# Turning the state by four full transposes, one half for both heads, and an earlier second half of the merge

## The chip, the cores and the metric

The kernel runs on one core of a Trainium2 chip. A core has a matrix engine (TensorE, "PE" in the profile, with its weight loads as "PEld"), three engines for element work (VectorE "DVE", ScalarE "ACT", GpSimd "POOL"), and SyncE ("SP"), from whose queue nearly all transfers of this kernel are issued. Each engine works through its own list of instructions; semaphores tie the lists together. The metric is the device time of one execution in microseconds, lower being better. TensorE writes its results to PSUM[...]; the other data live in SBUF.

## The reference, cut to what matters

The first half is a linear attention with a state of 40 x 40 per head (4 batches, 8 heads, 768 steps); the second is a mixture of four small networks, applied to the first half's output, all in float32:

```python
for t in range(S):
    y[:, :, t] = np.einsum('bhd,bhde->bhe', rt, state)
    Sa = np.einsum('bhde,bhe->bhd', state, at)
    state_decay = state * wt[:, :, None, :] - np.einsum('bhd,bhe->bhde', Sa, bt)
    state = state_decay + np.einsum('bhd,bhe->bhde', vt, kt)
...
p = domain_probs / (domain_probs.sum(-1, keepdims=True) + 1e-09)
for e in range(E):                      # 4 networks
    h = np.maximum(x @ w1[e], 0.0)      # (3072, 320) @ (320, 1024)
    out += p[:, e:e + 1] * (h @ w2[e])  # (3072, 1024) @ (1024, 320)
```

## The kernel before, in words

**Tiling.** Time is cut into 12 chunks of 64 steps. A *unit* is one chunk of two batches, so there are 24; two units in a row share a chunk. Inside a chunk the recurrence is written with matrices: scores between the 64 steps, a triangular system that is inverted, and the carried state. The 8 heads form four pairs (index j, head s within the pair), the two batches are index i, so a product has 16 blocks of up to 64 x 64. `quadrants` (L370) issues these on the four 64 x 64 quarters of TensorE, in an order given as a list of (j, s, i). A float32 matmul shows as two records in the profile, a transpose as one.

**Stages of a unit.** They are Python generators, advanced by the main loop with `run(generator, n)`:

- `within` (L389), two units ahead. The decays are turned and multiplied up (G, L400 to L410); pg turns them (L416); gp is its scaled reciprocal (L418, L419); n_tok and k_tok (L455, L459) are b and k scaled by it; A, V and R are turned 32 x 32 on VectorE (AT, VT, RT, by L228); pNT and pKT (L441) turn n_tok and k_tok; pc (L448) has the scores of values and receptances, pfe and pe those of a, n and k; EV (L516) is a first right-hand side.
- `substitute` (L523) inverts 32 x 32 triangles. VectorE makes M (L534 to L550) from copies of F (L528), then for all but the first two units GpSimd runs 48 steps on Z (L559, L572). That is the longest serial piece in a unit.
- `merge` (L578) joins two 32 x 32 inverses to one of 64 x 64. Its first part turns Z to Qc and QTc on VectorE (L583, L585) and copies to QT on GpSimd (L591); then pY (L609) with four ScalarE copies to Yq, then pQ (L612) with four to QT (L606).
- `step` (L615) carries the state. prn holds two results in the same two PSUM banks: the state times AT, added to EV to give RH (L633), and the state turned (psn, by products with the identity), which ScalarE copies to SN (L638). Then psat and its copies SaT, SX (L654, L659); pxr and its copies RS (L679); pdy, which gives the outputs Y (L694, L699) and the new state (L704, L705). From the third chunk on Y goes to xT, the input of the mixture, by twelve DMAs on SP's queue (L723).

**The mixture.** `mixture_of_chunk` (L836) puts pieces on a list: up-projections (ph, L738 for the last 64 rows of the weights in 64 x 64 quarters, L752 for the rest, ScalarE's hs L757, with w1 pieces reloaded from memory each time into w1p) and down-projections (p, L873, seven products in place of eight, from sums of hs on VectorE, a, L867; weighted sums osb L773). The main loop (L1057) runs four stretches of a unit's steps, and after each calls `gap(n)`, which takes up to two pieces off that list, so that TensorE has mixture work while other engines work on the recurrence. `lead()` issues the L738 part of the next up-projection ahead of its piece.

**What sets the order.** Inside an engine's list, a tile scheduler decides by its own estimate of times, except where `tc.keep_in_program_order` pins an instruction to its place in the program. The matmuls' results share a ring of five PSUM banks (`big`, L72) and one of three ("mm"); a matmul into a bank waits until the bank's last reader is done.

**The steady main loop before the change** (u from 5): pe, pxr; gap 0; pg, pev, pdy; gap 1; pNT, pKT, pc, prn with both results, pY; gap 2; pQ, pfe, the lead, psat; substitution of the next unit begins; gap 3. In terms of what stands around the change, from L1097: `run(w, 2)` (pNT to pc), `run(s_next, 1)` (prn), `run(m, 1)` (pY), `gap(2)`, `run(m, 1)` (pQ).

**Where a pair's heads stand.** Turned values and receptances have 128 partitions: in one half of 64 stands one head's 40 numbers, in the other another's. Before, `d_half(j, s)` (L357) puts head s of pair j in half s XOR (j mod 2), so the two heads of a pair lie in different halves, and `of_d_half` picks slots 0 and 3, or 1 and 2, of each group of four.

## Time and profile before

| | before |
|---|---|
| median of 3 runs | 1132.29 us (1129.44 to 1134.07) |
| profiled execution | 1129.6 us |
| its span on the core | 1127.5 us |
| granted TensorE clock, mean | 0.986 |
| TensorE busy (matmuls / weight loads) | 1083.1 us (96%) / 963.2 us (85%) |
| VectorE, GpSimd, ScalarE busy | 758.8, 498.8, 353.0 us |
| memory traffic | 111.79 MB read, 3.93 MB written |

The rows of the page come from one profiled execution. A row of the groups or of the timeline has the line of the program, the engine, the operation, the tile written and those read, sizes, and how often; in brackets, or after the last bar, stands the idle time of that engine just before, with what ended it. Rows of waits read "who waits <- for whom: us in total, times, longest us". Matmuls are pipelined: the length of one record says less than the distance between two starts.

### The profile page before, as it was taken

What the parts mean: (1) busy time and instruction counts of PE and PEld (TensorE: products, weight loads), DVE (VectorE), ACT (ScalarE), POOL (GpSimd) and SP (SyncE); (2) the same over time, 40 slices, a digit from 0 to 9 for tenths busy, and PEclk for the clock granted to TensorE, in tenths of its full rate; (3) what the DMA queues carried; (4) which work ended last, traced back from release to release, by engine and by line L of the source; (5) the groups of instructions that cost most, each with busy time, mean ns of one, the idle gap of its engine ahead of it and who ended that gap; (6) DMA issues with size and microseconds to landing.
All of it is one profiled execution on the core that took longest, in us unless ns stands there. A gap on an engine that the chain in (4) does not pass through costs nothing.

```text
span 1127.5 us, 38551 instructions
## 1 busy us (share of the span) xinstructions
PE 1083.1 (96%) x16100; PEld 963.2 (85%) x16100; DVE 758.8 (67%) x1553; ACT 353.0 (31%) x956; POOL 498.8 (44%) x1272
## 2 busy tenths in 40 slices
PE   6899997999999999999999999999999999999998
PEld 5777776788989889988989989989899999888887
DVE  8766547797766767677677677677677686553343
ACT  2323423332332332432432332332333323321110
POOL 5005727754625526437437347346346356340000
PEclk7899998999999999999999999999999999999999
DMA  7784553245253543644543543544553442231320
GB/s 118 214 239 125 130 113 71 71 108 126 77 130 88 122 102 99 141 103 93 143 104 88 143 103 90 142 96 96 133 114 86 122 110 63 76 90 57 108 90 12
DMA packets 268868, 122.18 MB, mean 108 GB/s; under 512 B 213736, under 2 KB 242072, under 8 KB 268696
## 3 DMA queue, kind: packets, MB, share of 16 engines
q1 hardware_dynamic: 265416, 119.12, 43.4%
q8 instruction: 127, 2.08, 0.8%
q10 hardware_dynamic: 3280, 0.61, 0.3%
q14 instruction: 45, 0.37, 0.1%
HBM read 111.79 MB, written 3.93 MB: 103 GB/s over the span
## 4 chain that ended last, share of the span: by engine, by line
PE 67%; POOL 10%; DVE 7%; issue 4%; ACT 2%; SPq 1%; DMA 1%; DVEq 0%; POOLq 0%
PE p L873 23%; PE ph L752 22%; PE ph L738 7%; POOL Z L572 6%; POOL Z L559 4%; PE pdy L376 2%; PE psat L376 2%; PE po L796 2%; DVE M L534 1%; PE pxr L376 1%; PE prn L376 1%; PE pQ L599 1%; PE pfe L376 1%; DVE G L406 1%; PE pc L376 1%
## 5 line engine op out<-in xcount | busy, mean ns | idle before, releaser
L752 PE MATMUL ph<-xT,w1p 128*128 128x256 f32 (+1 forms) x1520 | 342.7, 378 | 1.7 <-issue 1.7
L752 PEld LDWEIGHTS ph<-xT,w1p 128*128 128x128 f32 x1520 | 273.4, 190 | 63.1 <-issue 25.6
L572 POOL TENSOR_TENSOR Z<-Z 128x31 f32<-128x31 f32 (+7 forms) x704 | 257.2, 365 | 55.2
L867 DVE TENSOR_TENSOR a<-hs 128x512 f32<-128x512 f32 x220 | 153.8, 716 | 104.6 <-ACT hs L757 104.6
L559 POOL TENSOR_TENSOR Z<-M,Z 128x62 f32<-128x62 f32 (+7 forms) x352 | 144.0, 409 | 134.5 <-DVE M L550 108.7
L757 ACT ACTIVATE hs<-ph 128x512 f32<-128x512 f32 (+1 forms) x208 | 115.3, 564 | 235.3 <-PE ph L752 234.3
L873 PE MATMUL p<-sums,a 128*128 128x160 f32 x1056 | 165.1, 299 | 0.0
L873 PEld LDWEIGHTS p<-sums,a 128*128 128x128 f32 x1056 | 152.9, 190 | 2.3
L773 DVE SCALAR_TENSOR_TENSOR osb<-p,gate,osb 128x320 f32<-128x320 f32 (+1 forms) x243 | 107.9, 482 | 55.3 <-PE p L873 52.1
L531 POOL COPY below<-F 32x256 f32<-32x256 f32 x48 | 23.4, 488 | 219.5 <-ACT F L489 217.8
L738 PE MATMUL ph<-xT,w1p 64*64 64x256 f32 (+1 forms) x1520 | 111.1, 379 | 5.4 <-issue 5.4
L873 PE MATMUL p<-w,a 128*128 128x160 f32 x704 | 105.8, 301 | 0.9 <-ACT hs L757 0.5
L873 PE MATMUL p<-w,hs 128*128 128x160 f32 x704 | 102.9, 299 | 0.0
L873 PEld LDWEIGHTS p<-w,hs 128*128 128x128 f32 x704 | 100.3, 190 | 2.2
L873 PEld LDWEIGHTS p<-w,a 128*128 128x128 f32 x704 | 98.3, 190 | 3.6 <-ACT hs L757 3.6
L591 POOL COPY QT<-QTc 32x256 f32<-32x256 f32 x96 | 49.3, 513 | 91.4 <-DVE QTc L585 44.9
L738 PEld LDWEIGHTS ph<-xT,w1p 64*64 64x64 f32 x1520 | 66.1, 135 | 14.3 <-issue 9.8
L534 DVE STREAM_TRANSPOSE M<-blocks 128x1024 f32<-128x1024 f32 x24 | 47.2, 1968 | 33.9 <-ACT blocks L528 33.7
L679 ACT COPY RS<-pxr 64x256 f32<-64x256 f32 x88 | 32.2, 366 | 115.0 <-DVE SX L387 73.6
L419 DVE RECIPROCAL gp<-gp 128x320 f32<-128x320 f32 x24 | 51.7, 2153 | 0.8
L516 ACT COPY EV<-pev 64x160 f32<-64x160 f32 x96 | 23.4, 286 | 88.1 <-PE pev L376 87.7
L583 DVE STREAM_TRANSPOSE Qc<-Z 128x256 f32<-128x256 f32 x24 | 15.1, 631 | 49.1 <-POOL Z L572 48.9
(151 smaller groups left out, 1427.9 us busy)
## 6 DMA issues: line engine op xcount, KB each, us to landing
w1p<-in_moe_w_dram SPq DMA_DIRECT2D x95, 512.0 KB
w1p<-in_moe_w_dram SPq DMA_DIRECT2D x190, 64.0 KB
w<-in_moe_w_dram SPq DMA_DIRECT2D x4, 1280.0 KB
sums<-in_moe_w_dram SPq DMA_DIRECT2D x9, 512.0 KB
natW<-in_w_dram SPq DMA_DIRECT2D x48, 80.0 KB
natB<-in_b_dram SPq DMA_DIRECT2D x48, 80.0 KB
natK<-in_k_dram SPq DMA_DIRECT2D x48, 80.0 KB
out_dram<-osb SPq DMA_DIRECT2D x46, 80.0 KB
```

The lines of the kernel that those rows point to most:

```text
L376: nc.tensor.matmul(out=p[row][half(col), lo + at * out_cols:lo + (at + 1) * out_cols], lhsT=lhsT, rhs=rhs, start=(n == 0), stop=(n == len( ...
L419: pin(nc.vector.reciprocal(out=gp[:], in_=gp[:]))
L534: ins = nc.vector.transpose(out=M[:], in_=cols)
L559: ins = eng.tensor_tensor(out=Z[:, 1:3, 0:n, j + 1:Q], in0=M[:, j:j + 2, None, j + 1:Q].to_broadcast([P, 2, n, m]), in1=Z[:, here, 0:n, j: ...
L572: eng.tensor_tensor(out=z[:, 0], in0=z[:, 0], in1=z[:, x], op=ALU.add)
L591: ins = nc.gpsimd.tensor_copy(out=q.QT[quarter(i), :, quarter(i % 2)], in_=QTc[quarter(i)])
L738: nc.tensor.matmul(out=ph[i][half(c), f, :], lhsT=w1.last[part(i), f, half(c)], rhs=xT[part(i), 2, :], start=(f == 0), stop=False,)
L752: nc.tensor.matmul(out=ph[i][:, f, :], lhsT=w1.main[:, g, at * P:(at + 1) * P], rhs=xT[:, g, :], start=False, stop=(g == 1 and f == HF // ...
L757: nc.scalar.activation(out=h[:, i * HF // 2:(i + 1) * HF // 2, 0:n], in_=ph[i][:], func=ACTF.Relu,)
L773: nc.vector.scalar_tensor_tensor(out=to, in0=p, scalar=sc, in1=to, op0=ALU.mult, op1=ALU.add)
L867: nc.vector.tensor_tensor(out=t[:], in0=x, in1=y, op=op)
L873: nc.tensor.matmul(out=p[:, n * HD:(n + 1) * HD], lhsT=a[:, f, :], rhs=b[:, f, :], start=(f == 0), stop=(f == HF - 1),)
```

## The change

Four edits, with what follows from them in the tiles:

1. The carried state is turned by four float32 transposes of 128 x 128 (`turn_state`), one for two pairs of one batch, instead of sixteen quarter matmuls with the identity. They are issued after pg, in the stretch before the unit's own, into one PSUM bank of their own; one ScalarE copy of 128 x 512 makes SN (a tile with one buffer of its own) in place of two of 128 x 256. The ring "step" falls from three buffers to two.
2. Both heads of a pair of turned values and receptances (and of what is multiplied with them) lie in the same half: the half is j mod 2, the slot 2 (j div 2) + s. The loads, pc, psat, pxr and the masks follow; the copies of pxr to RS become two of 128 partitions in place of four of 64. In the first three units, where V and R are turned on TensorE, there are four copies each in place of three.
3. For u from 5, pY and prh (the rest of prn) are issued ahead of pc, and pQ is issued before gap 2 in place of after it.
4. A `lead()` puts the L738 part of gap 2's up-projection ahead of pQ.

The diff, cut to its core:

```diff
@@ load_raw
-                    sets = ((slice(0, 8, 2), slice(r, 16, 4)), (slice(1, 8, 2), slice(3 - r, 16, 4)))
+                    sets = [(slice(y, 8, 2), slice(2 * r + y, 16, 4)) for y in range(2)]
@@ helpers
-    def d_half(j, s):
-        return s ^ (j % 2)
+    def of_d(x, j, s, i, n=64):
+        return x[64 * (j % 2):64 * (j % 2) + n, 4 * i + 2 * (j // 2) + s, :]
...
-    BY_PAIRS = [(2 * j + x, s, i) for i in range(2) for j in range(2) for s, x in QUADS]
+    BY_D_TOKENS = [(2 * jj + r, s, i) for jj in range(2) for s in range(2) for r, i in QUADS]
+    BY_TOKENS_D = [(2 * jj + x, s, r ^ s) for jj in range(2) for s in range(2) for r, x in QUADS]
+    BY_D_HEADS = [(2 * jj + r, s, i) for jj in range(2) for i in range(2) for r, s in QUADS]
@@ before step
+    def turn_state(q):
+
+        if q.start:
+            return
+        psn = big("psn")
+        for i in range(2):
+            for jj in range(2):
+                x = state[q.b[i]][:, 2 * jj:2 * jj + 2, :].rearrange("p j d -> p (j d)")
+                at = (2 * i + jj) * P
+                nc.tensor.transpose(out=psn[:, at:at + P], in_=x, identity=ident[:])
+        q.SN = sb.tile([P, 2, 2, 2, 64], FP32, name="SN", tag="SN", bufs=1)
+        nc.scalar.copy(out=q.SN[:].rearrange("p i jj s e -> p (i jj s e)"), in_=psn[:])
@@ step
-            psn = quadrants(p, NJ * D, BY_PAIRS, 64, lambda j, s, i: (
-                s, d_half(j, s), 2 * i + j // 2, st[i][half(s), j, :], ident[half(s), half(s)],
-            ))
...
-            SN = sb.tile([P, 2, 2 * 2, 64], FP32, name="SN", tag="step", bufs=3)
-            for s in range(2):
-                nc.scalar.copy(out=SN[:, s], in_=psn[s])
...
             for x in range(2):
-                for s in range(2):
-                    nc.scalar.copy(
-                        out=RS[half(s), x ^ s::2], in_=prs[x][half(s)].rearrange("p (j i) t -> p j i t", i=2),
-                    )
+                nc.scalar.copy(out=RS[:, x::2], in_=prs[x].rearrange("p (jj i) t -> p jj i t", i=2))
@@ main loop
         run(w, 1)
+        if u + 1 < NU:
+            turn_state(units[u + 1])
         if not early:
             run(w_next)
         run(s)
...
-        run(w, 2)
+        run(w, 1)
+        if not early:
+            run(m, 1)
+            run(s_next, 1)
+        run(w, 1)
...
         if early:
             run(m, 1)
         else:
-            run(s_next, 1)
+            lead()
             run(m, 1)
         if soon:
             substitute(units[u + 2], nc.gpsimd)
         gap(2)
 
-        if not early:
-            run(m, 1)
         if not soon:
             run(w, 1)
```

More of the change, by code (lines that the diff above doesn't have):

```diff
@@ L355, in head @@
         return 2 * j + s
-    def d_half(j, s):
-        return s ^ (j % 2)
+    def of_d(x, j, s, i, n=64):
+        return x[64 * (j % 2):64 * (j % 2) + n, 4 * i + 2 * (j // 2) + s, :]
     def of_d_half(x, r):
-        return x.rearrange("p (jj four) e -> p jj four e", four=4)[:, :, slice(1, 3) if r else slice(0, 4, 3), :]
+        return x.rearrange("p (jj four) e -> p jj four e", four=4)[:, :, 2 * r:2 * r + 2, :]
     BY_TOKENS = [(j, s, i) for j in range(NJ) for s, i in QUADS]
-    BY_PAIRS = [(2 * j + x, s, i) for i in range(2) for j in range(2) for s, x in QUADS]
+    BY_D_TOKENS = [(2 * jj + r, s, i) for jj in range(2) for s in range(2) for r, i in QUADS]
+    BY_TOKENS_D = [(2 * jj + x, s, r ^ s) for jj in range(2) for s in range(2) for r, x in QUADS]
+    BY_D_HEADS = [(2 * jj + r, s, i) for jj in range(2) for i in range(2) for r, s in QUADS]
     def banks(name):
@@ L428, in turn_rv @@
                 p = turn(f"p{x}T", tok(n["padded" + x]), q.u == 1)[:].rearrange("p (j i t) -> p j i t", i=2, t=L)
-                to = t[:].rearrange("p (i j) t -> p j i t", i=2)
-                nc.scalar.copy(out=to[:, 0::2], in_=p[:, 0::2])
+                to = t[:].rearrange("p (i jj s) t -> p s jj i t", i=2, s=2)
                 for r in range(2):
-                    nc.scalar.copy(out=to[half(r), 1::2], in_=p[half(1 - r), 1::2])
+                    for y in range(2):
+                        nc.scalar.copy(out=to[half(r), y], in_=p[half(y), r::2])
             return VT
@@ L447, in causal_scores @@
         def causal_scores(VT):
-            pc = quadrants(banks("pc"), 0, BY_TOKENS, L, lambda j, s, i: (
-                d_half(j, s), i, j, of_slots(VT, d_half(j, s), j, i, D), of_slots(q.RT, d_half(j, s), j, i, D),
+            pc = quadrants(banks("pc"), 0, BY_D_TOKENS, L, lambda j, s, i: (
+                j % 2, i, 2 * (j // 2) + s, of_d(VT, j, s, i, D), of_d(q.RT, j, s, i, D),
             ))
@@ L622, in step @@
         else:
-            p = banks("prn")
-            prh = quadrants(p, 0, BY_TOKENS, D, lambda j, s, i: (
+            prh = quadrants(banks("prh"), 0, BY_TOKENS, D, lambda j, s, i: (
                 s, i ^ s, j, of_slots(q.AT, s, j, i), st[i][half(s), j, 0:D],
-            ))
-            psn = quadrants(p, NJ * D, BY_PAIRS, 64, lambda j, s, i: (
-                s, d_half(j, s), 2 * i + j // 2, st[i][half(s), j, :], ident[half(s), half(s)],
             ))
@@ L635, in step @@
                 )
-            SN = sb.tile([P, 2, 2 * 2, 64], FP32, name="SN", tag="step", bufs=3)
-            for s in range(2):
-                nc.scalar.copy(out=SN[:, s], in_=psn[s])
         yield
         p = banks("psat")
-        psa = quadrants(p, 0, BY_TOKENS, L, lambda j, s, i: (
-            i ^ s, d_half(j, s), j, RH[half(i ^ s), head(j, s), :], q.QT[half(i ^ s), head(j, s), :],
+        psa = quadrants(p, 0, BY_TOKENS_D, L, lambda j, s, i: (
+            i ^ s, j % 2, 2 * (j // 2) + s, RH[half(i ^ s), head(j, s), :], q.QT[half(i ^ s), head(j, s), :],
         ))
@@ L651, in step @@
             ))
-        SaT = sb.tile([P, NJ, 2, L], FP32, name="SaT", tag="step", bufs=3)
+        SaT = sb.tile([P, NJ, 2, L], FP32, name="SaT", tag="step", bufs=2)
         for x in range(2):
@@ L662, in step @@
         p = banks("pxr")
-        px = quadrants(p, 0, BY_TOKENS, L, lambda j, s, i: (
-            d_half(j, s), i, j, SaT[half(d_half(j, s)), j, i ^ s, :], of_slots(q.RT, d_half(j, s), j, i),
+        px = quadrants(p, 0, BY_D_TOKENS, L, lambda j, s, i: (
+            j % 2, i, 2 * (j // 2) + s, SaT[half(j % 2), 2 * (j // 2) + s, i ^ s, :], of_d(q.RT, j, s, i),
         ))
         if not q.start:
-            prs = quadrants(p, NJ * L, BY_PAIRS, L, lambda j, s, i: (
-                d_half(j, s), s, 2 * (j // 2) + i, SN[half(d_half(j, s)), s, 2 * i + j // 2, :],
-                of_slots(q.RT, d_half(j, s), j, i),
+            prs = quadrants(p, NJ * L, BY_D_HEADS, L, lambda j, s, i: (
+                j % 2, s, 2 * (j // 2) + i, q.SN[half(j % 2), i, j // 2, s, :], of_d(q.RT, j, s, i),
             ))
@@ L675, in step @@
         if not q.start:
-            RS = sb.tile([P, NJ, 2, L], FP32, name="RS", tag="step", bufs=3)
+            RS = sb.tile([P, NJ, 2, L], FP32, name="RS", tag="step", bufs=2)
             for x in range(2):
-                for s in range(2):
-                    nc.scalar.copy(
-                        out=RS[half(s), x ^ s::2], in_=prs[x][half(s)].rearrange("p (j i) t -> p j i t", i=2),
-                    )
+                nc.scalar.copy(out=RS[:, x::2], in_=prs[x].rearrange("p (jj i) t -> p jj i t", i=2))
         yield
@@ L690, in step @@
         )
-        Y = sb.tile([P, NJ, 2, L], FP32, name="Y", tag="step", bufs=3)
+        Y = sb.tile([P, NJ, 2, L], FP32, name="Y", tag="step", bufs=2)
         Gv = q.G.rearrange("p (j i) t -> p j i t", i=2)
```

## The prediction

> **What bounds the kernel now.** I read the page first, parts 1, 2 and 4.

> ```profile
> PE 1083.1 (96%) x16100; PEld 963.2 (85%) x16100; DVE 758.8 (67%) x1553; ACT 353.0 (31%) x956; POOL 498.8 (44%) x1272
> PE   6899997999999999999999999999999999999998
> PE 67%; POOL 10%; DVE 7%; issue 4%; ACT 2%; SPq 1%; DMA 1%; DVEq 0%; POOLq 0%
> ```

> TensorE is full after the first fifth, and most of the ending chain is its own work: matmuls run back to back, so each microsecond it waits in the steady part is added to the time. Next the waits, for what is just in time.

> ```profile
> ACT SN L638 <- DVE RH L633: 74.6, 21, 5.4
> DVE Qc L583 <- POOL Z L572: 48.9, 20, 6.0
> PE pY L599 <- DVE QTc L585: 5.8, 4, 3.4
> ```

> VectorE waits some 2.4 us per unit at the head of its queue for GpSimd's substitution (Z) before it can transpose it (Qc); TensorE hardly notices. Why shows on the timelines of TensorE and then VectorE (start, length, what).

> ```profile
> 561.53 0.60 PE L340 MATMUL pg<-ident,G 128*128 128x128 f32 x4
> 562.06 0.68 PE L376 MATMUL pev<-VC,ET 64*64 64x40 f32 x32
> ...
> 571.94 0.60 PE L340 MATMUL pNT<-ident,n_tok 128*128 128x128 f32 x4
> 572.38 0.60 PE L340 MATMUL pKT<-ident,k_tok 128*128 128x128 f32 x4
> 572.91 0.70 PE L376 MATMUL pc<-RT,VT 40*64 40x64 f32 x32
> 573.42 0.63 PE L376 MATMUL prn<-state,AT 64*64 64x40 f32 x32
> 573.86 0.67 PE L376 MATMUL prn<-ident,state 64*64 64x64 f32 x32
> 574.36 0.57 PE L599 MATMUL pY<-QTc,below 64*64 64x64 f32 x13
> ```

> I time a unit from the start of pg. pNT starts at 10.41 in every steady unit, pc at 11.38, pY at 12.83; units take 42.74 to 43.24. In the unit whose pg starts at 604.39, VectorE did:

> ```profile
> 608.54 0.66 DVE L228 STREAM_TRANSPOSE RT<-rawR 128x512 f32<-128x512 f32 x1
> 609.12 0.72 DVE L694 TENSOR_TENSOR Y<-pdy,RS 128x256 f32<-128x256 f32 x2
> ...
> 611.36 0.48 DVE L455 SCALAR_TENSOR_TENSOR n_tok<-natB,gp 128x320 f32<-128x320 f32 x1
> ...
> 612.09 0.65 DVE L459 TENSOR_TENSOR k_tok<-natK,gp 128x320 f32<-128x320 f32 x1
> 615.13 0.64 DVE L583 STREAM_TRANSPOSE Qc<-Z 128x256 f32<-128x256 f32 x1 [2.39 <-POOL Z L572]
> 615.62 0.41 DVE L228 STREAM_TRANSPOSE G<-rawW 128x256 f32<-128x256 f32 x1
> 615.94 0.40 DVE L585 STREAM_TRANSPOSE QTc<-Qc 128x256 f32<-128x256 f32 x1
> ```

> n_tok, which pNT needs, ends at 7.45; k_tok at 8.35; Qc starts at 10.74, when Z is done; QTc ends at 11.95, before pY. Nothing that TensorE needs before pY stands behind Qc.

> [...]the 2.39 us at Qc agrees, later instructions did not overtake it. [...]the trace has 0.39 us of "issue" idleness where 128x128 ph loads follow 64x64 ones, and 32 records per unit for the state turned in quadrants against four for a 128x128 transpose. [...]in the trace the Z steps under n_tok and k_tok run 0.33, 0.23 and 0.13 us over their usual pitch.

> **The change, part by part.** *State.* Sixteen quadrant matmuls, 32 records, go: 573.86 to 574.36, 0.50 us per unit. Four transposes are added; pNT to pKT gives four in 0.44. They stand beside pg[...]: -0.06. But psn's PSUM bank passes to the second bank of pdy (this is in the built order and its waits), which now waits for ScalarE's copy of 128x512 (0.59, the row of KT). psn ends 1.04 after pg, the copy at 1.67, pdy's second bank is due at 1.55: +0.2. Behind it on TensorE stand pdy and the up-projection; ScalarE was idle there, so its queue (the EV copies, needed much later) may slip 0.6 at no cost.

> *Halves.* R and V are loaded with as many DMAs of the same sizes on SP's queue. The RS copies fall from four of 366 ns to two, off TensorE's path: 0, hidden by 8 us that ScalarE idled before RS. Units 0 to 2 get one ScalarE copy more for each of V and R: 6 x 0.37, at most 2 us, partly hidden.

> *Merge and SN.* SN no longer stands between Yq and hs in ScalarE's queue behind RH; p26 then no longer waits for hs. pfe came at 22.66 in three steady units and 22.88 to 23.22 in the rest, so -0.3. pQ's eight matmuls only move, and Yq (four copies, 1.09) is ready: pY 12.0 to 12.4, copies 12.7 to 13.8, pQ due at 14.2. Its copies to QT go ahead of hs instead of ahead of F: 0. Per unit: -0.06 + 0.2 - 0.3, about -0.2; over 13 steady units -2.6.

> *The order on VectorE.* The built order of the changed kernel differs in seven units, every second one from the unit of 432.78 on:

> ```
> before: gp reciprocal RT Y Y state Y state state n_tok state k_tok Qc G QTc
> after:  gp reciprocal RT Qc Y Y state Y state state n_tok state k_tok QTc
> ```

> Qc is hoisted over everything that pNT needs, while Z is no earlier. Z starts from M, which follows psat by 3.9 us through ScalarE's copies (24.34 to 28.25), lasts 25.4 with its start-up, and pg follows psat by 18.5: Z ends at 3.9 + 25.4 - 18.5 = 10.8 however the unit shifts. Take off the 0.69[...], since VectorE now idles there: 10.1. Qc starts then, Y 0.5 later, n_tok ends 2.72 after that (609.12 to 611.84): 13.3. pNT is due at 10.41 + 0.44 + 0.2 = 11.05, so TensorE stands 2.25. k_tok ends 0.9 later, at 14.2; pKT is due at 13.75: 0.48 more. QTc (14.55) is in time for pY (14.75). Seven times 2.73 is 19.1.

> What is late next: Y, so its twelve xT DMAs on SP, and w1p behind them.

> ```profile
> 610.82 9.36 SPq L723 DMA_DIRECT2D xT<-Y  x12
> 620.29 1.66 SPq L287 DMA_DIRECT2D w1p<-in_moe_w_dram  x3
> ```

> xT starts 1.70 after Y: 12.25; w1p is issued at 21.7. The matmuls on it are due at 22.7 + 0.5 + 2.7 = 26.0, 4.3 us later. The tightest such pair before was 5.9 without a stall, and one w1p in the chain took 4.70: 0 to 1.6, I take 0.3, seven times, +2. xT itself lands in time, as do natB, natK and rawW behind it, needed a unit later.

> In four of the other units RT now stands before Y; its last DMA is issued at 4.3 to 4.9 there and must land, k_tok shifts to 11.2 to 12, Qc with it, and pY, due at 12.0 now, waits about 0.5: 4 x 0.5, and 0.1 in two more, +2.2. If RT's data are early this is 0.6 in all.

> Sum: -2.6 + 19.1 + 2 + 2.2 = +20.7, and 0 +- 3 for the first 430 us, where other waits (DMA, VectorE) rule. On the profiled execution of 1129.6 (its span of 1127.5 plus 2.1) this gives 1150.3; it lies 2.7 under the median of 1132.29, so on medians 1153.

> **Rivals.** *The wait is hidden.* If Qc's new place costs nothing, only the small gains remain: about -0.2 in 20 units, 1128. Z would have to end by 11.05 - 2.72 - 0.5 = 7.8 for that, 3 us before any steady unit shows it; for this, only that the order was chosen at all. This is the other side, and it decides at 7.8.

> *The wait is smaller.* [...]a delayed unit gives back part of its stall: 1.2 us per stall instead of 2.7, 1142. The trace speaks against a return: from pY on TensorE is full.

> *The clock drops.* [...]The trace shows both: after 2.2 us of idleness at 179.5 the 128x128 transposes took 421 ns for 275, after 2.3 at 369.2 nothing changed. A half-clock spell costs some 1.7 us (the windows of 100 to 200 us lose 3 at a clock of 0.97). In all seven: +11, 1164.

> *w1p is late.* 1.6 in each of seven, with the upper ends of RT: +10, 1163. That the change does not do what it says is no case: the built order has the four transposes, two RS copies and pQ ahead of the up-projection.

> **How the numbers follow.** Qc's place as worked out 0.66; smaller 0.12; hidden or faster 0.09; clock 0.09; w1p 0.04. The predicted time is that of the first, 1153, its own range 1147 to 1159 (stall 2.0 to 3.4). The 8 in 10 reach to 1138 and 1163. Half a per cent, 5.7 us, is what a measurement tells here: faster than 1126.6 gets 0.06, within 0.09 (some of "hidden", the edge of "smaller"), slower 0.85.

> **What would show it.** In the changed profile the wait of pNT and pKT for VectorE's n_tok and k_tok should read some 19 us in seven pairs, Qc's wait for Z lengthen to about 5 us in those units, and psn's four transposes take 0.44. Waits of pdy for ScalarE's SN should be 0.1 to 0.3 each; pY for QTc a few in the RT units. If pNT never waits, the forecast is wrong; if units without Qc hoisted don't get 0.2 shorter, the gains are.

## The result, and the profile after it

The changed kernel takes 1158.01 us in the median of 6 runs (1156.21 to 1161.31), the kernel before 1133.24 beside it (6 runs, 1129.44 to 1135.38). The ratio is 1.0226, with a 95% interval of 1.0203 to 1.0248: slower by 2.3%, 24.8 us. The prediction was 1153, with 1138 to 1163 as its range. The profiled execution took 1160.05 us, with a span of 1157.9 against 1127.5 before and a mean TensorE clock of 0.979 against 0.986.

First the page of the changed kernel: part 1, the TensorE slices of part 2, and the engines in the chain that ended last.

```profile
PE 1095.9 (95%) x15484; PEld 973.5 (84%) x15484; DVE 757.1 (65%) x1553; ACT 339.0 (29%) x896; POOL 492.1 (43%) x1272
PE   6799997999999998999999999999999999999998
PE 54%; POOL 19%; DVE 8%; issue 5%; ACT 2%; DMA 2%; SPq 1%; DVEq 0%; POOLq 0%
```

TensorE has 616 records fewer and still takes 30 us longer. The slices hide that, since one of them covers 29 us; the chain does not: GpSimd's Z went from 10% to 19% of it, TensorE from 67% to 54%. The waits (engine and line that waited, what it waited for, us in all, times, longest) say where:

```profile
ACT SN L628 <- PE psn L626: 75.0, 21, 4.6
DVE Qc L585 <- POOL Z L574: 58.8, 20, 5.6
...
PE pNT L340 <- DVE n_tok L457: 15.1, 9, 2.3
...
PE pY L601 <- DVE QTc L587: 5.9, 7, 2.2
...
PE ph L741 <- DMA w1p<-in_moe_w_dram: 3.5, 4, 1.9
```

SN no longer waits for RH, but for its own psn. Qc waits 10 us more for Z in all, and two waits have appeared that the prediction named: pNT for n_tok, and ph for its weights. The unit whose pg starts at 616.36 shows both. TensorE's timeline (start, length, what, and in brackets the idle time before it and its releaser):

```profile
616.36 0.60 PE L340 MATMUL pg<-ident,G 128*128 128x128 f32 x4
616.79 0.60 PE L626 MATMUL psn<-ident,state 128*128 128x128 f32 x4
617.32 0.68 PE L378 MATMUL pev<-VC,ET 64*64 64x40 f32 x32
...
629.29 0.66 PE L340 MATMUL pNT<-ident,n_tok 128*128 128x128 f32 x4 [1.69 <-DVE n_tok L457]
630.01 0.63 PE L340 MATMUL pKT<-ident,k_tok 128*128 128x128 f32 x4
```

The four transposes cost 0.43 (pev starts 0.96 after pg, for 0.53 before). pNT starts at 12.93 after pg. In the units that do not stall it starts at 11.07. VectorE in the same unit:

```profile
621.29 0.66 DVE L228 STREAM_TRANSPOSE RT<-rawR 128x512 f32<-128x512 f32 x1
626.33 0.62 DVE L585 STREAM_TRANSPOSE Qc<-Z 128x256 f32<-128x256 f32 x1 [4.39 <-POOL Z L574]
626.81 0.72 DVE L697 TENSOR_TENSOR Y<-pdy,RS 128x256 f32<-128x256 f32 x2
...
628.75 0.48 DVE L457 SCALAR_TENSOR_TENSOR n_tok<-natB,gp 128x320 f32<-128x320 f32 x1
...
629.38 0.48 DVE L461 TENSOR_TENSOR k_tok<-natK,gp 128x320 f32<-128x320 f32 x1
629.78 0.44 DVE L587 STREAM_TRANSPOSE QTc<-Qc 128x256 f32<-128x256 f32 x1
```

Qc stands ahead of Y, waits 4.39 us for Z and holds everything behind it: Y starts 10.46 after pg, for 4.73 in the unit shown of before. With Y, xT is late. SP's queue and then TensorE at the next ph:

```profile
628.39 10.80 SPq L726 DMA_DIRECT2D xT<-Y  x12
639.30 1.66 SPq L287 DMA_DIRECT2D w1p<-in_moe_w_dram  x3
```

```profile
641.44 0.69 PE L378 MATMUL pfe<-NT,AT 64*64 64x64 f32 x32
644.01 1.19 PE L741 MATMUL ph<-xT,w1p 64*64 64x256 f32 x13 [1.87 <-DMA w1p<-in_moe_w_dram]
```

w1p is issued 22.94 after pg (15.90 before), and its first matmul starts 4.71 later. The same view of SP's waits, of the kernel before and then of the changed one, has the whole shift in a line; xT waits for Y, and the line names the state update that VectorE runs beside it:

```profile
SPq L723 <- DVE state L704: 32.3, 11, 7.5
```

```profile
SPq L726 <- DVE state L707: 72.3, 13, 12.6
```

That is 40 us more, 5.7 for each of seven units. TensorE's waits show only 3.5 of it, as ph's for w1p, yet it is the line that mattered most, as the experiments show.

The first of the seven units, at 433.0, is a case of its own. ph begins there, stops after two records and waits 3.66, and the profile names no releaser. It is not w1p: the last of its three loads had landed (its semaphore was complete) 5.6 after the first was issued, before ph began. VectorE, and then TensorE:

```profile
460.03 0.71 DVE L228 STREAM_TRANSPOSE AT<-rawA 128x512 f32<-128x512 f32 x1 [7.75 <-DMA rawA<-in_a_dram]
464.05 0.37 DVE L776 SCALAR_TENSOR_TENSOR osb<-p,minus_gate,osb 128x160 f32<-128x160 f32 x1
464.53 1.32 PE L741 MATMUL ph<-xT,w1p 64*64 64x256 f32 x11 [3.66 <-issue]
```

ph goes on 0.11 after this osb ends. In the run with Qc put back (below) the same wait is 1.34 and ends 0.10 after the same osb, and in fill_gap (below) the profile names osb as its releaser. That ph waits for osb to free a PSUM bank is my reading. What makes it late is shown: VectorE waits 7.75 us for rawA, one more load that stands behind xT on SP's queue; with Qc put back it waits 4.47.

An account of the seven units, against the run in which Qc is put back (below). The second column is pNT's start after pg, 11.07 where nothing is late; the fourth counts the spells of 3.41 us in which TensorE's granted clock was 0.50.

```
pg at    pNT     idle before ph   half clock   period   with Qc put back
433.0   13.02        3.66             2        52.33       44.75
528.0   12.99        0.28             0        45.66       42.91
616.4   12.93        1.87             0        47.17       42.77
706.2   13.13        0                1        46.70       42.83
795.6   13.13        0                1        46.65       43.17
886.1   12.06        0.91             0        45.32       42.95
974.3   12.99        0.40             0       183.65*     179.69*    (* to the end)
```

pNT's delays sum to 12.8 and pKT's further 0.29 each to 2.0. ph's waits for w1p are 3.5, and the wait in the first unit is 2.3 longer than with Qc put back. A spell costs 1.6: from pNT's start to pfe's it is 13.7 to 13.8 in the three units where a spell falls between, and 12.2 in the unit of 528.0 without; four at that price make 6.3. Together 26.9; the periods differ by 28.4, and of the 1.5 left over 1.4 lies in the last stretch, which runs to the end. The account does not yet say what each part would give back, since parts that follow one another can hide one another.

### The profile page after: what moved, and what is told of

It is laid out like the page before. It is cut to its first block, busy times and chain, and to the rows that moved or that the text cites. A ratio compares the mean times of both kernels' runs of the same rounds, so it can differ in the third digit from the quotient of the medians.

```text
span 1157.9 us, 37229 instructions
## 1 busy us (share of the span) xinstructions
PE 1095.9 (95%) x15484; PEld 973.5 (84%) x15484; DVE 757.1 (65%) x1553; ACT 339.0 (29%) x896; POOL 492.1 (43%) x1272
## 4 chain that ended last, share of the span: by engine, by line
PE 54%; POOL 19%; DVE 8%; issue 5%; ACT 2%; DMA 2%; SPq 1%; DVEq 0%; POOLq 0%
PE ph L755 18%; PE p L876 17%; POOL Z L574 12%; POOL Z L561 7%; PE ph L741 6%; DVE M L536 2%; PE psat L378 2%; DMA w1p<-in_moe_w_dram 2%; PE pdy L378 2%; PE po L799 1%; SPq L726 1%; PE pY L601 1%; PE pc L378 1%; PE pxr L378 1%; PE prh L378 1%
## 5 line engine op out<-in xcount | busy, mean ns | idle before, releaser
L574 POOL TENSOR_TENSOR Z<-Z 128x31 f32<-128x31 f32 (+7 forms) x704 | 247.6, 352 | 55.2
L561 POOL TENSOR_TENSOR Z<-M,Z 128x62 f32<-128x62 f32 (+7 forms) x352 | 148.7, 422 | 154.1 <-DVE M L552 128.2
L741 PE MATMUL ph<-xT,w1p 64*64 64x256 f32 (+1 forms) x1520 | 116.4, 382 | 9.9 <-issue 6.3
L876 PE MATMUL p<-w,a 128*128 128x160 f32 x704 | 103.2, 299 | 0.6 <-ACT hs L760 0.6
L741 PEld LDWEIGHTS ph<-xT,w1p 64*64 64x64 f32 x1520 | 66.8, 136 | 22.3 <-issue 13.8
L585 DVE STREAM_TRANSPOSE Qc<-Z 128x256 f32<-128x256 f32 x24 | 15.1, 629 | 58.9 <-POOL Z L574 58.8
L684 ACT COPY RS<-pxr 128x256 f32<-128x256 f32 x44 | 15.5, 372 | 128.7 <-DVE SX L389 75.1
L378 PE MATMUL pdy<-SX,n_tok 64*64 64x104 f32 (+1 forms) x768 | 40.8, 247 | 2.9 <-DVE SX L389 2.9
```

What stands on the lines that cost most here:

```text
L378: nc.tensor.matmul(out=p[row][half(col), lo + at * out_cols:lo + (at + 1) * out_cols], lhsT=lhsT, rhs=rhs, start=(n == 0), stop=(n == len( ...
L561: ins = eng.tensor_tensor(out=Z[:, 1:3, 0:n, j + 1:Q], in0=M[:, j:j + 2, None, j + 1:Q].to_broadcast([P, 2, n, m]), in1=Z[:, here, 0:n, j: ...
L574: eng.tensor_tensor(out=z[:, 0], in0=z[:, 0], in1=z[:, x], op=ALU.add)
L741: nc.tensor.matmul(out=ph[i][half(c), f, :], lhsT=w1.last[part(i), f, half(c)], rhs=xT[part(i), 2, :], start=(f == 0), stop=False,)
L876: nc.tensor.matmul(out=p[:, n * HD:(n + 1) * HD], lhsT=a[:, f, :], rhs=b[:, f, :], start=(f == 0), stop=(f == HF - 1),)
```

## The experiments

Times are medians, in us; each ratio is to the kernel before on the same chip (1133.2 to 1134.1 there), with its 95% interval.

```
run                   time     ratio    interval           what
qc_behind            1132.01   0.9997   0.9981 to 1.0013   changed, Qc behind k_tok
psn_late             1130.98   0.9977   0.9963 to 0.9991   changed, psn behind pdy
hoist_before         1164.51   1.0296   1.0261 to 1.0330   before, with the new order on VectorE
tokens_late          1140.19   1.0052   1.0036 to 1.0069   before, n_tok and k_tok behind Qc
y_late               1152.72   1.0163   1.0131 to 1.0194   before, Y and state behind Qc
changed_tokens_late  1135.62   1.0023   1.0006 to 1.0039   changed, only n_tok and k_tok behind Qc
changed_y_late       1154.70   1.0185   1.0160 to 1.0210   changed, only Y and state behind Qc
fill_gap             1160.67   1.0253   1.0229 to 1.0277   changed, filler ahead of pNT
hoist_fill           1170.34   1.0327   1.0295 to 1.0358   hoist_before, filler ahead of pNT
merge_only           1142.53   1.0075   1.0047 to 1.0103   before, merge edit alone
no_merge             1128.41   0.9968   0.9954 to 0.9982   qc_behind without the merge edit
psn_ahead            1126.68   0.9944   0.9930 to 0.9959   no_merge, psn ahead of pg
```

**Is the order on VectorE the loss?** In both built orders Qc stands behind RT's transpose, the instruction traced just before it on VectorE; nothing in the program ties it to Y or k_tok. The first experiment adds that tie in every steady unit, an order of issue without a semaphore:

```diff
-        tc.keep_in_program_order(nc.vector.transpose(out=dealt(Qc[:]), in_=q.Z))
+        ins = tc.keep_in_program_order(nc.vector.transpose(out=dealt(Qc[:]), in_=q.Z))
+        if q.apart:
+            tc.add_manual_dep(ins.ins, newest_k[-1].ins.name, ..., reason="behind k_tok")
```

> The changed kernel with one edit: in every steady unit VectorE's Qc is queued behind the newest k_tok, as it was in the kernel before (built order of the seven units: gp reciprocal, RT, Y, Y, state, Y, state, state, n_tok, state, k_tok, Qc, G, QTc). Transposes of the state, halves and the merge stay as changed. Theory (the order on VectorE is the whole loss): all stalls of pNT and pKT go, the late xT and w1p and the clock spells behind them go too, and what is left are the small gains of 0.2 in some 13 units: 1130.6, that is 1128 to 1133.5 against 1133 for the kernel before. Rival (the new transposes, the wait of pdy for SN and the moved merge cost more than was counted): the time stays at 1140 or above, and units without the stall are no shorter than before. A time of 1134 to 1140 would put a part of the loss on each.

Measured: 1132.01. The whole loss of 24.8 us goes with this edge, and what is left is no change that can be measured. VectorE's timeline of this run has n_tok ending 6.7 to 9.7 after pg in the steady units, and pNT at 11.07 in all. TensorE in the unit that stands where that of 616.36 stood:

```profile
609.58 0.60 PE L340 MATMUL pg<-ident,G 128*128 128x128 f32 x4
...
620.66 0.60 PE L340 MATMUL pNT<-ident,n_tok 128*128 128x128 f32 x4
...
633.01 1.24 PE L749 MATMUL ph<-xT,w1p 64*64 64x256 f32 x16
```

The second asks why the scheduler moved Qc at all. It moves the call of turn_state and nothing else:

```diff
         run(w, 1)
-        if u + 1 < NU:
-            turn_state(units[u + 1])
         if not early:
             run(w_next)
         run(s)
+        if u + 1 < NU:
+            turn_state(units[u + 1])
```

> The changed kernel with the call of turn_state moved from just behind pg to just behind pdy. Nothing else is edited, but the built order of VectorE is then that of the kernel before in all seven units (Qc behind k_tok), so the wait of pdy for SN is what had let the scheduler put Qc first. Theory: the stalls go as in the kernel with Qc queued behind k_tok; the wait of pdy for SN (0.2) goes too, but psn now stands alone between 64x64 pdy and 64x64 ph, so two changes of tiling are added, 0 to 0.4 each, and psn may wait some tenths for its PSUM bank: 1127 to 1138, I take 1131. Rival (the four transposes themselves cost, wherever they stand): 1140 or more.

Measured: 1130.98. The 0 to 0.4 for a change of tiling was an estimate from the 0.39 us for which TensorE's weight loads stood idle at such a change in the kernel before (at 565.12); this run does not isolate it. With psn behind pdy, pdy's bank no longer waits for SN, and the built order of VectorE is the old one without any edge. So the wait that the prediction priced at 0.2 us per unit probably had a second effect through the builder: Y came later in its reckoning, later than Qc in every second unit. That is argued and not shown: the builder's reckoning is not on record, and this run moves psn's place as well as its wait.

The third puts the cause into the kernel before. Edges queue Y, the state, n_tok and k_tok of seven units behind Qc; TensorE's, ScalarE's, GpSimd's and SP's orders stay what they were.

```diff
+        if q.u in HOISTED:    # range(10, 23, 2)
+            for x in units[q.u - 1].step_ops + units[q.u + 1].token_ops:
+                tc.add_manual_dep(x.ins, ins.ins.name, ..., reason="behind Qc")
```

> The kernel before with one edit: in seven units (every second one) Y, the state, n_tok and k_tok are queued behind Qc on VectorE, which gives the very order of the changed kernel (gp reciprocal, RT, Qc, Y, Y, state, Y, state, state, n_tok, state, k_tok, QTc). Theory (the order alone is the loss, whatever else is changed): pNT is due at 10.4 without the transposes and the SN wait, so it stalls 0.65 longer than in the changed kernel, 2.9, and pKT 0.5; seven times 3.4 is 24, and w1p and the clock add 0 to 10: 1157 to 1167. Rival (the order costs only together with the other edits): below 1146.

Measured: 1164.51, 31 us slower.

```profile
615.56 0.60 PE L341 MATMUL pg<-ident,G 128*128 128x128 f32 x4
628.67 0.63 PE L341 MATMUL pNT<-ident,n_tok 128*128 128x128 f32 x4 [2.53 <-DVE n_tok L456]
```

The order is enough by itself. It costs more here than in the changed kernel: pNT, due 0.65 earlier, waits 2.4 to 2.5 in six units (1.4 in the other), p then waits 6.1 in all for hs, and four half-clock spells follow the waits of pNT (the mean clock of that profile is 0.979, for 0.986 in the kernel before). ph never waits for w1p here; it comes late enough without.

**The stall or the late Y?** Behind Qc stand two groups: n_tok and k_tok, for which pNT and pKT wait, and Y, for which xT and the loads behind it wait. The same edges, for one group at a time, first on the kernel before:

```diff
-            for x in units[q.u - 1].step_ops + units[q.u + 1].token_ops:
+            for x in units[q.u + 1].token_ops:        # tokens_late
+            for x in units[q.u - 1].step_ops:         # y_late
```

> The kernel before with one edit: in the seven units n_tok and k_tok alone are queued behind Qc on VectorE; Y and the state keep their place ahead of it, so xT and the w1p load behind it leave at their usual time. Theory (the stall and the late Y are two losses, and both count): only the stall is here. Z ends at about 10.5 (Y and the state still collide with it), n_tok some 1.5 later, pNT is due at 10.4: a stall of 1.6 and 0.2 at pKT, seven times 1.8 is 13, no half-clock spell since no gap is over 1.7: 1143 to 1149. Rival (the late Y makes most of the loss): 1140 or less.

> The kernel before with one edit: in the seven units Y and the state alone are queued behind Qc on VectorE; n_tok and k_tok go ahead of it, so pNT and pKT should not wait. xT is issued some 6 us later than in the kernel before, and w1p behind it. Theory of the prediction (w1p late costs 0 to 1.6, 0.3 on average): 1133 to 1140. Rival (in the changed kernel the stall of 2.7 us ahead of it hides most of w1p's lateness; with no stall ahead it shows in full, as waits of ph for w1p): 2 to 4 us in each of seven, 1147 to 1160. That would say that undoing the stall without moving Y back gains nothing.

Measured: 1140.19 and 1152.72. The stall was smaller than I expected, 1.1 to 1.2 at pNT in each of seven: n_tok starts as soon as Qc is through. The expected end of Z counted on slower steps beside Y and the state: the one of 128x98 took 0.70 us there in the kernel before (unit of 604.39), and 0.37 in the changed kernel with VectorE waiting. The seven sum to 7.8, so they cover that run's loss of 6.1. The late Y alone costs 18.6. But in this kernel its waits are not those of the changed one: pc and prn wait 0.7 per unit for the state update to free pdy's banks, and p waits 1.0 for hs, which stands behind SN and RH. So the pair was repeated on the changed kernel, where SN has left that queue. In both runs with a late Y the builder also moved some loads on SP's queue.

> The changed kernel with one edit on VectorE: in the seven units Qc is queued behind Y and the state, and only n_tok and k_tok stay behind it; in the other steady units Qc is behind all of them. Y, xT and the loads behind xT leave at their old time. From the run on the kernel before: Qc at 10.4, n_tok ends at 11.5, k_tok at 11.9; pNT is due at 11.07 and pKT at 12.0 here, so each of the seven units stalls 0.5, against 2.7 in the changed kernel. Theory (what remains of the loss beyond this stall comes from Y being late): 1132 + 7 x 0.5 = 1135.5, 1133 to 1139. Rival (Qc's place costs in some other way): above 1142.

> The changed kernel with the other edit on VectorE: in the seven units n_tok and k_tok go ahead of Qc, and only Y and the state stay behind it. pNT and pKT do not wait. Theory of the loads (xT is issued 6 us late, w1p, natB, natK, rawW, rawV and rawR stand behind it on SP's queue, and the waits for them grow by what the stall no longer hides): the time stays near that of the changed kernel, 1148 to 1158, with waits of ph for w1p of 2 us or more in most of the seven units. Theory of the stall (pNT's wait of 2.7 us is the cost and w1p adds 0.3, as the prediction had it): 1133 to 1140.

Measured: 1135.62 and 1154.70. With Y back in its place and the tokens still behind Qc, pNT waits 0.2 to 0.6 in six of the seven units, for 1.7 to 1.9 in six of the changed kernel, and 22.4 of the 24.8 us are back. TensorE in one of these:

```profile
616.54 0.66 PE L341 MATMUL pNT<-ident,n_tok 128*128 128x128 f32 x4 [0.58 <-DVE n_tok L458]
```

With the tokens back in place and Y still late, pNT never waits, pY waits 1.1 to 1.4 for QTc instead, and only 3.3 us are back. SP's waits and TensorE at the ph of one unit in that run:

```profile
SPq L741 <- DVE QTc L600: 51.2, 7, 13.5
```

```profile
636.36 0.69 PE L379 MATMUL pfe<-NT,AT 64*64 64x64 f32 x32
638.90 1.10 PE L756 MATMUL ph<-xT,w1p 64*64 64x256 f32 x13 [1.85 <-DMA w1p<-in_moe_w_dram]
```

This is the answer. In the seven units of that run w1p is issued 21.4 to 22.2 after pg, and ph waits in all seven, until 26.2 to 27.0: 4.7 to 4.9 after the issue each time. The profile names w1p in only three of the seven and other events in four, but in all seven ph starts 0.1 to 0.4 after the second of w1p's three loads has landed. In the changed kernel the four waits for w1p end 4.6 to 4.8 after the issue. In the run with Qc put back this ph starts at 23.5. So a Y behind Qc sets a floor under ph at about 21.6 + 4.7 = 26.3, 2.8 us late, and 7 x 2.8 = 19.6 of the loss, by this estimate, is there whether pNT stalls or not. The stall of 2.2 runs down inside that floor. What comes over it is at most the 3.3 us between the two runs. In the profiles even that is elsewhere: the six later units, each counted as in the table, take 415 us together in both, and the first takes 45.87 for 52.33, since the builder had here issued all of rawA ahead of xT, so that VectorE does not wait for it.

Two things were not run. One is the changed kernel with w1p issued ahead of xT, which would show the loads' part without touching VectorE. The other is a stall of 2.2 with Y in time: changed_tokens_late shrinks the stall too, so 22.4 is not the price of Y alone. From tokens_late, where 7.8 of waits at pNT cost 6.1, I estimate 9 for the 11.6 of such waits in the changed kernel. Either late group alone would then be dear, and the two overlap; which of them is the larger part depends on which is undone first.

**The half-clock spells.** Filler on TensorE, transposes of the identity into pNT's own bank, 16 in the changed kernel and 12 in hoist_before, in the seven units:

```diff
         p = big(name)
+        for n in range(fill):
+            ins = nc.tensor.transpose(out=p[:, 0:P], in_=ident[:], identity=ident[:])
         for j in range(NJ):
```

> The changed kernel with sixteen idle 128x128 transposes of the identity put ahead of pNT on TensorE in the seven units of the stall; they write pNT's own bank and fill some 1.76 us of the wait for n_tok. VectorE's order, with Qc ahead of Y, stays. Theory (clock): the half-clock spells of 3.4 us that follow three of the seven gaps in the trace (and one gap before ph) come from TensorE's idleness; with the gap filled they do not come, and the time falls by 3 x 1.7 = 5, to 1153 (1151 to 1155). Rival (the spells come from something else, or the extra time of those units is another wait): 1157 to 1160. If the filler doesn't fit in the gap, pNT is late by what sticks out, up to 0.3 each, +2.

> The kernel before with the hoisted order (Y, state, n_tok and k_tok behind Qc in seven units), measured before at 1164.5, and now twelve idle 128x128 transposes of the identity ahead of pNT in those units: 1.3 us of the gap of 2.5 is filled, and 1.2 of idleness is left. The builder orders some loads and one VT a little differently. Theory (half-clock spells follow when TensorE idles for half of a 3.4 us period): the four spells behind the gaps of pNT go, 4 x 1.7 = 7: 1155 to 1160. Rival (the spells don't come from the gap, or what they cost is waited for elsewhere): 1162 to 1167.

Measured: 1160.67 and 1170.34, neither faster than the kernel it was put into. The mean granted clock was 0.979 to 0.984 over fill_gap's four runs, for 0.979 to 0.982 over the changed kernel's six, and 0.976 to 0.982 over hoist_fill's four, for 0.975 to 0.979 over hoist_before's: 0.001 and 0.002 more on average, which I estimate at 1.5 and 2.3 us of clock in 1160. The time did not fall; hoist_fill lies above even the rival's range. In fill_gap the idle time before ph is longer in the first unit (4.3 for 3.7) and in hoist_fill p waits 11.7 for hs where it waited 6.1. Both tests have a flaw: the builder also reordered some loads and moved VT. In fill_gap VectorE now had

```profile
705.71 0.71 DVE L228 STREAM_TRANSPOSE VT<-rawV 128x512 f32<-128x512 f32 x1 [5.29 <-DMA rawV<-in_v_dram]
706.35 0.73 DVE L393 COPY_PREDICATED SX<-mask_up,pxr 128x256 f32<-128x256 int32 x2
```

with SX, RS, hs and p behind that wait. So what the spells are worth is open. One sign says less than 1.6 each: the units with a spell in the changed kernel (46.70 and 46.65) are 1.0 longer than the one without a spell and nearly without idle time at ph (45.66). That filling the gaps gave no time back fits this and shows no more, since which spells went is not known.

**The edits one by one.**

```diff
-        run(w, 2)
+        run(w, 1)
+        if not early:
+            run(m, 1)
+            run(s_next, 1)
+        run(w, 1)
...
         else:
-            run(s_next, 1)
+            lead()
             run(m, 1)
...
-        if not early:
-            run(m, 1)
```

This is the merge edit, put alone into the kernel before (merge_only), or undone in qc_behind (no_merge):

> The kernel before with the third edit alone: second half of the merge one stretch forward, step ahead of it, the lead of the up-projection behind it. State in quadrants and the old halves stay. VectorE's order has Qc behind k_tok in all units. Theory (the gain of 0.2 to 0.3 per unit comes from this part, since p26 no longer waits for hs behind SN): 1128 to 1132. Rival (it comes from the four transposes, or there is none): 1132.5 to 1136.

> The changed kernel without its third edit (the merge's second half and the step stand where they stood before), with Qc queued behind k_tok in all units, so that this is the state by transposes and the new halves alone, without the stall. Theory: pY comes 0.64 - 0.50 = 0.14 later than in the kernel before, p26 does not wait 0.23 for hs since SN has left ScalarE's queue, and psat keeps its 0.2 that the early QT takes off in the changed kernel: -0.1 per unit, 1131 to 1135. With merge alone measured at 1142.5, this would say that the two edits do not add: the transposes beside pg fill the 0.65 that pY waits for QTc in the kernel with the merge alone. Rival (the transposes cost by themselves): 1137 or more.

Measured: 1142.53 and 1128.41; both expectations missed. Alone, the merge edit costs 8.4. TensorE in that run:

```profile
582.07 0.60 PE L340 MATMUL pKT<-ident,k_tok 128*128 128x128 f32 x4
583.67 0.59 PE L599 MATMUL pY<-QTc,below 64*64 64x64 f32 x13 [1.00 <-DVE QTc L585]
```

With pY moved ahead of pc and prn, nothing lies between pKT and pY, which then waits 0.6 to 1.0 for QTc, and so for Z, in every steady unit. In qc_behind, where psn has pushed pKT 0.65 later, the wait is 0 to 0.4. Without the merge edit pY starts at 13.0, a microsecond after QTc, never waits, and the period is 42.57 and 42.8 by turns, for 42.7 to 43.2 before. This is 0.32% faster than before. The halves were not tried apart from the state, so the gain belongs to the two together.

That leaves pdy's wait for SN, which psn ahead of pg removes. The edit puts the call of turn_state one line up, ahead of run(w, 1):

> The kernel of the run without the merge edit (state by transposes, new halves, Qc behind k_tok; measured at 1128.4), with turn_state moved ahead of pg: psn's four transposes come before pg's, so ScalarE's copy of SN is through by the time the second bank of pdy is due. One difference: the wait of pdy for SN. Theory (step 2 of the prediction priced it at 0.2 per unit): 0.2 in some 14 steady units is 3: 1124.5 to 1127, and pNT comes 0.2 earlier in each unit counted from psn. Rival (the wait is covered, or the later pg makes n_tok, Y and the loads behind it late by 0.44): 1128 to 1131.

Measured: 1126.68, 0.9944 of the kernel before (0.9930 to 0.9959), and faster than both kernels by more than the measurement is uncertain. TensorE in one unit:

```profile
561.16 0.60 PE L634 MATMUL psn<-ident,state 128*128 128x128 f32 x4
561.60 0.60 PE L340 MATMUL pg<-ident,G 128*128 128x128 f32 x4
...
572.01 0.60 PE L340 MATMUL pNT<-ident,n_tok 128*128 128x128 f32 x4
```

From psn to pNT it is 10.85, where no_merge has 11.07 from pg to pNT with the same work in between: the 0.2 of step 2. The period is 42.35 and 42.6 in most units, again 0.2 less. The ratios of no_merge and psn_ahead, 0.9968 and 0.9944, have intervals that overlap at the edge; the timeline is what shows this step.

## Why the prediction was right, and where it was not

**The state.** psn was priced at 0.44, and takes 0.43. pNT was put at 10.41 + 0.44 + 0.2 = 11.05; it stands at 11.07 in every unit without a stall. The wait for SN is the 0.2 that psn_ahead got back.

**Merge and SN.** The sum of -0.2 per unit was right, the shares were not. The gain fits SN's leaving ScalarE's queue, which the state edit does and not the merge edit: sixteen records of p (L873) that wait for hs take 2.57 or more in the kernel before and 2.34 in no_merge. no_merge has all of the gain and more, 3.6 us by its ratio. The merge edit was counted as free ("pQ's eight matmuls only move") and costs: qc_behind against no_merge is 1132.0 to 1128.4, with intervals that just touch, and merge_only shows it clearly. pY did come at 12.0 to 12.4, as predicted. The step that failed is that TensorE is through with pKT by 12.04, so that all beyond it is a wait; the prediction put it at nothing.

**Qc's place.** Right in kind and place: seven units, Qc at 10.0 to 10.2 (10.1 predicted; 9.1 in one), pNT and pKT waiting. The size was 2.73 per unit and measured 2.15, as pfe's shift from 23.0 to 25.15. The mis-sized term is Y to n_tok's end: 2.72 was taken from the kernel before, where these operations ran beside Z; with Z over, Qc's start to n_tok's end takes 2.9 for 3.2, k_tok 0.48 for 0.65. So the traces show both engines slower side by side: three of Z's steps, of 128x98, 128x49 and 128x35, took 0.70 us (beside Y and the state), 0.52 (n_tok and the state) and 0.40 (k_tok) in the kernel before and 0.37, 0.29 and 0.27 in the changed one, where VectorE waited at Qc. The prediction had counted this for Z alone, and put the first step under n_tok. Seven stalls were to be 19.1 and were 14.8.

**w1p late.** The prediction named it and gave it 0.3 each, 2 in all, with 1.6 as the upper end; the trace has 3.5 in all, 0 to 1.9 in six units. Of the other loads behind xT the prediction named natB, natK and rawW and left out rawA, which made a wait 2.3 longer in the first unit. As a sum, in order of time, stall and then what w1p adds is right, and only the sizes were off. What the prediction did not see is how little of this sum the stall decides. With its own figures, w1p issued at 21.7 and 4.7 to its first matmul make 26.4, against 23.2 (22.7 + 0.5) without a stall: a late Y alone costs 3.2 per unit, 22 us in seven. The runs show that: with Y late and no stall at pNT 21.5 of the 24.8 are there. An engineer who had read the prediction and moved n_tok and k_tok back would have gained 3 us.

**RT.** 2.2 was foreseen for pY waiting in four units; pY waited 0.25 and 0.17 in two of them and not in the others. k_tok ended at 9.6 to 10.6, not at 11.2 to 12: the last load of rawR was issued at 3.1 to 4.3, not at 4.3 to 4.9. The lower end, 0.6, was right.

**The rivals.** "The clock drops" came true in part, three spells behind the seven stalls of pNT and one behind a wait of ph, and so did "w1p is late". That the sum came within 5 us is in part luck. In the account above the spells (6.3, put at nothing in the sum), w1p (1.5 more) and rawA (2.3) were too cheap, and the small gains were put 1 to 2 too large; against that the stalls were 4.3 and RT 1.6 too dear. "Hidden" was wrong as expected: Z ended at 9.1 at the earliest, and it had to be 7.8.

## What to carry to other kernels

When an instruction that waits is moved up an engine's queue, list everything it now holds back (nothing behind Qc started on VectorE in the 2.56 to 5.25 us that it waited in the seven units) and follow each item to its last user. Here undoing the visible stall (n_tok) gave back 3 us, and undoing what only fed a queue of loads (Y) gave back 22, in part because it shortened the stall too. Idle times do not show this, because two delays on one path hide each other; a run that undoes one of them shows what it is worth while the other stands, and no more. A new PSUM wait of 0.2 us may be enough for a scheduler to reorder another engine, so compare the built orders after every change of a bank, and tie an instruction that waits long to what must go ahead of it. And a step moved forward is only free if what lay between it and its input moves along.

## What the hardware showed

The time from the issue of a w1p load (three DMAs, 640 KB) to the first matmul that was waiting for it was 4.6 to 4.8 us in the four cases of the changed kernel and 4.7 to 4.9 in the seven of changed_y_late. In the first of the changed kernel's seven units the last of the three landed 5.6 us after the first was issued. So it is no constant, but it is the kind of number to hold against the slack of such a load.
